# One attention-plus-two-layers kernel: conversion jobs in another order, more filler transposes at the start, the last product's operands split in place

## Chip, cores and metric

The kernel runs on one core of one Trainium2 chip. The metric is device time in microseconds; the time before is the median of three runs, 1113.74 us (1110.79 to 1116.33).

## What is computed

The reference is attention with rotary embedding, then a gated layer with a norm in front, then a second layer without a nonlinearity. Shapes: batch 4, 8 heads, 576 positions, 64 per head; 2304 tokens of width 512; inner widths 1536 and 1024.

```
q_rot, k_rot = rotate(q), rotate(k)
attn = softmax(q_rot @ k_rot.T / sqrt(64)) @ v            # 32 heads
x  = attn as [2304, 512]
xn = x / sqrt(mean(x*x) + 1e-6) * rms_g
x2 = (silu(xn @ w_gate) * (xn @ w_val)) @ w_out            # gated layer
h  = (x2 @ w1) * (x2 @ w2) @ w3                            # second layer
out = h @ w_out2
```

All inputs are double-width words, of which the kernel makes 32-bit floats itself. Each operand of a product is split into a high part (rounded to the multiplier's format) and a low part (the remainder), and every product is three passes: high·high, high·low, low·high (`PASS`).

## The kernel before

**Start and attention.** A core has TensorE (PE, with its weight loads PEld), VectorE (DVE), ScalarE (ACT), GpSimd (POOL), and SyncE (SP), whose one queue issues all the DMAs. The work goes by 16 pairs of heads; pair 0's start is written out by hand (lines 705 to 753). `warm(i)` issues `WARM[i]` transposes of the identity into a bank that nobody reads: 22 before anything else, 2 after the transposes `q2p` of the rotated keys, 3 after `q0p`. Then come `q1p`, the splits into `xy`, copies into `ks` and `qs`, and the first scores (L495). ACT takes the exponential (L506) after DVE's maximum (L500). The keys and queries of pair 1 go into `ks` and `qs` by DMA (`move`, L447). The order in attention is a table (`ORDER`, `ONCE`) and is not touched.

**Gated layer.** The tokens go in six chunks of 384. A step is one slice of 128 inner columns of one chunk: 24 matmuls into `mm` (L307), then ACT's silu `sg` (L317), DVE's product `u` (L319), and the split of `u` into `us`, high by ACT (L106), low by DVE (L107). The 12 matmuls that add `us` times `w_out` into `acc` (L828) come one step later. Chunks 0 and 1 convert the layer's own weights; from chunk 2 on DVE, ACT and SP prepare the second layer in **jobs**, which the list `JOBS` hangs on steps (i, n), chunk and slice:

- `job_wo` (8 of them): load 512 KB of `w_out2`, convert (`conv`: one ACT step L856, three DVE steps L857, L860, L861), split by ACT and DVE, store two parts in `woD`.
- `job_w3` (16): load, convert, store one part in `w3D`.
- `job_ws` (8): convert `w1` or `w2` and store sums of blocks in `wsD` for a seven-product scheme.
- `job_sums` (4): read two chunks' `x2` back, form block sums, split them, store in `xsD`. Its `xo` tiles are in the pool `x2` of three buffers, which the tiles `xr` of the norm (of the next chunk) and the results `x` share.

A job's load is issued a step or more ahead of its work. A scheduler sets the order of each engine's queue from the program's order, dependencies and modelled times; DVE, ACT and SP then take their queues strictly in order.

**Second layer and end.** Stage L1064 forms the seven products per block; its chains of matmuls add into a bank that ACT (L1070 to L1078) or DVE (L1054) must read in between. Its operands `xs` leave the pools `xsA` and `xsB` as the last blocks finish. Into the freed slots go `woc` (`w_out2`, both parts, from `woD`). `w3_trans` transposes a block of `w3` (L1156) and splits it (L106, L107); `w3_prod` multiplies it with all eight `woc` (L1167) and splits the result into `wp`. Then `load_us` loads the layer's `u` from `uD` into a `gv` tile and splits it into `us`, chunk by chunk, and L1205 makes the output of a chunk in 72 matmuls. `load_us(0)` stands after all eight `w3_prod`.

Of the kernel before, what the change touches and what calls it, by code (L numbers as in the profile page):

```python
# [8 lines left out]
F32 = mybir.dt.float32  # L9
# [31 lines left out]
WARM = (22, 2, 3, 17)  # L41
# [8 lines left out]
JOBS = ([(2, 0, ("wo", 0)), (2, 1, ("wo", 1))] + [(2, 3 + j, ("wo", j)) for j in range(2, 8)] + [(2, 11, ("w3", 0, 0))]  # L50
        + [(3, j // 2 if j < 10 else j - 5, ("w3", (j + 1) // 2, (j + 1) % 2)) for j in range(15)]
        + [(i, 2 + c, ("sums", i // 2 - 1, c)) for i in (2, 4) for c in range(2)]
# [10 lines left out]
def f(ap):  # L63
    return ap.bitcast(F32)
# [3 lines left out]
def kernel(  # L68
# [56 lines left out]
    woD = dram.tile([128, NJ, 2, DM], F32, name="woD")  # L125
# [598 lines left out]
    def warm(i):  # L724
        for _ in range(WARM[i]):
            nc.tensor.transpose(wps[:, 0:128], idn, idn)
# [10 lines left out]
    for i, n_ in enumerate(("q2p", "q0p", "q1p")):  # L737
        part[n_](0)
        if i < 2:
            warm(i + 1)  # L740
# [128 lines left out]
    def job_wo(j):  # L869
        load, rest = conv(rows(w_out2, j))  # L870

        def go():
            t = rest()
            hi, lo = [wt_p.tile([128, 512], F32R, tag="t", name="wt") for _ in range(2)]
            split(hi, lo, t)
            for i, o in enumerate((hi, lo)):
                nc.sync.dma_start(out=woD[:, j, i], in_=f(o))
        return [load, go]
# [150 lines left out]
    def gtile(shape, dt=F32):  # L1029
        return gv.tile(shape, dt, tag="g", name="gv")  # L1030
# [141 lines left out]
    def load_us(i):  # L1172
        us = []
        for g in range(NJ // 2):
            t = gtile([128, 2, CH])
            nc.sync.dma_start(out=t, in_=uD[:, 2 * g:2 * g + 2, i * CH:(i + 1) * CH])
            o = (xsA if i else xsB).tile([128, 2, 2, CH], F32R, tag="x", name="us")
            split(o[:, 0], o[:, 1], t)
            us.append(o)
        return us  # L1180
# [3 lines left out]
    for j in range(NJ):  # L1184
        woc[j] = (xsA if j < 7 else xsB).tile([128, 2, 512], F32R, tag="x", name="woc")
        nc.sync.dma_start(out=f(woc[j]), in_=woD[:, j])
    w3_trans(0)
    for j in range(NJ):
        if j + 2 < NJ:
            w3_load(j + 2)  # L1190
        if j + 1 < NJ:
            w3_trans(j + 1)
        w3_prod(j)


    nus = load_us(0)
# [74 lines left out]
```

## Time and profile before

| what | value |
|---|---|
| median of three runs | 1113.74 us (1110.79 to 1116.33) |
| the profiled execution's own time | 1111.08 us |
| its span in the trace | 1109.3 us |
| PE busy | 1075.6 us (97%) |
| DVE busy | 685.0 us (62%) |
| ACT busy | 558.2 us (50%) |
| POOL busy | 242.8 us (22%) |
| DMA, mean over the span | 165 GB/s |

The span is the profiled execution from its first to its last instruction; 1.8 us of its time lie around it. Shares of busy time are means over stages. Attention takes the span up to some 300 us, the gated layer from there to 775 us, the seven-product stage to 960 us, the last products the rest. In the trace's views a line is "start, length, engine, line, operation, out<-in, count", and what stands in brackets is the idle time ahead of it and what ended that.

### The profile page before, as it was taken

What the parts mean: (1) busy time and instruction counts of PE and PEld (TensorE: products, weight loads), DVE (VectorE), ACT (ScalarE), POOL (GpSimd) and SP (SyncE); (2) the same over time, 40 slices, a digit from 0 to 9 for tenths busy, and PEclk for the clock granted to TensorE, in tenths of its full rate; (3) what the DMA queues carried; (4) which work ended last, traced back from release to release, by engine and by line L of the source; (5) the groups of instructions that cost most, each with busy time, mean ns of one, the idle gap of its engine ahead of it and who ended that gap; (6) DMA issues with size and microseconds to landing.
All of it is one profiled execution on the core that took longest, in us unless ns stands there. A gap on an engine that the chain in (4) does not pass through costs nothing. (4 is left out here: it accounts for less than half of the span.)

```text
span 1109.3 us, 18452 instructions
## 1 busy us (share of the span) xinstructions
PE 1075.6 (97%) x6627; PEld 1036.1 (93%) x6627; DVE 685.0 (62%) x1278; ACT 558.2 (50%) x1241; POOL 242.8 (22%) x359
## 2 busy tenths in 40 slices
PE   6899999999899999999999999999999999999998
PEld 6899999999889999999999999999899999887886
DVE  6899999999889853452677566552363442423320
ACT  5799998998865533232533343233353433223230
POOL 5878898799300000000000000000000000000000
PEclk8999999999999999999999999999999999999999
DMA  7678867776356531151978685636932416604451
GB/s 201 168 179 205 211 173 187 197 195 149 85 181 182 170 95 58 41 169 43 310 242 286 213 285 197 219 101 206 349 112 71 134 72 197 221 15 127 143 171 57
DMA packets 124699, 183.53 MB, mean 165 GB/s; under 512 B 18624, under 2 KB 85696, under 8 KB 124608
## 3 DMA queue, kind: packets, MB, share of 16 engines
q1 hardware_dynamic: 124608, 182.35, 54.1%
q8 instruction: 53, 0.87, 0.3%
q14 instruction: 38, 0.31, 0.1%
HBM read 101.63 MB, written 52.17 MB: 139 GB/s over the span
## 5 line engine op out<-in xcount | busy, mean ns | idle before, releaser
L307 PE MATMUL mm<-xc,wgv 128*128 128x384 f32 x1728 | 316.4, 335 | 0.9 <-ACT sg L317 0.5
L307 PEld LDWEIGHTS mm<-xc,wgv 128*128 128x128 f32 x1728 | 299.9, 188 | 1.8 <-ACT wgv L244 0.9
L1064 PE MATMUL ps<-xs,cw 128*128 128x384 f32 x1008 | 176.5, 335 | 2.2 <-DMA xs<-xsD 2.2
L1064 PEld LDWEIGHTS ps<-xs,cw 128*128 128x128 f32 x1008 | 174.5, 188 | 3.6 <-DMA xs<-xsD 2.9
L828 PE MATMUL acc<-us,wo 128*128 128x384 f32 x864 | 167.3, 336 | 4.5 <-ACT us L106 2.6
L828 PEld LDWEIGHTS acc<-us,wo 128*128 128x128 f32 x864 | 150.6, 188 | 7.8 <-ACT us L106 4.2
L495 PE MATMUL s<-ks,qs 128*128 128x288 f32 x640 | 122.6, 319 | 10.8 <-ACT osb L573 5.6
L500 DVE TENSOR_REDUCE nm<-s 128x1 f32<-128x576 f32 x144 | 107.9, 749 | 10.8 <-PE s L495 9.0
L506 ACT ACTIVATE p<-s,nm 128x576 f32<-128x576 f32 x144 | 107.5, 747 | 12.8 <-DVE nm L500 12.2
L495 PEld LDWEIGHTS s<-ks,qs 128*128 128x128 f32 x640 | 91.9, 194 | 14.0 <-ACT osb L573 5.6
L1205 PE MATMUL ps<-wp,us 128*128 128x512 f32 x432 | 98.2, 389 | 1.4 <-ACT us L106 1.4
L1205 PEld LDWEIGHTS ps<-wp,us 128*128 128x128 f32 x432 | 81.0, 188 | 18.6 <-ACT us L106 1.8
L520 DVE TENSOR_TENSOR pt<-tp,pt 128x512 fp32r<-128x512 f32 x144 | 94.5, 681 | 1.2 <-ACT pt L516 0.6
L319 DVE SCALAR_TENSOR_TENSOR u<-mm,sg 128x384 f32<-128x384 f32 x72 | 39.8, 553 | 78.2 <-PE mm L307 70.4
L106 ACT CAST us<-u 128x384 fp32r<-128x384 f32 x72 | 36.8, 511 | 101.4 <-DVE u L319 101.1
L568 PE MATMUL pv<-pt,vs 128*128 128x288 f32 x512 | 81.0, 300 | 2.7 <-DVE pt L520 2.7
L516 ACT CAST pt<-tp 128x512 fp32r<-128x512 f32 x144 | 82.5, 585 | 1.4 <-PE tp L512 0.5
L512 PE MATMUL tp<-idn,p 128*128 128x128 f32 x576 | 82.1, 275 | 0.1
L568 PEld LDWEIGHTS pv<-pt,vs 128*128 128x128 f32 x512 | 70.8, 188 | 3.2 <-DVE pt L520 3.2
L512 PEld LDWEIGHTS tp<-idn,p 128*128 128x128 f32 x576 | 67.9, 142 | 1.4 <-issue 0.4
L317 ACT ACTIVATE sg<-mm 128x384 f32<-128x384 f32 x72 | 35.1, 488 | 54.9 <-PE mm L307 54.6
L1054 DVE TENSOR_TENSOR gv<-ps,gv 128x384 f32<-128x384 f32 x48 | 26.7, 556 | 53.5 <-PE ps L1064 33.4
(138 smaller groups left out, 1368.3 us busy)
## 6 DMA issues: line engine op xcount, KB each, us to landing
ks<-xy SPq DMA_DIRECT2D x62, 288.0 KB, 5.0
wraw<-in_moe_w_dram SPq DMA_DIRECT2D x32, 512.0 KB, 5.1
xsD<-xo SPq DMA_DIRECT2D x28, 384.0 KB, 3.6
xs<-xsD SPq DMA_DIRECT2D x14, 768.0 KB, 8.6
wraw<-in_moe_w_out_dram SPq DMA_DIRECT2D x20, 512.0 KB, 4.4
qs<-xy SPq DMA_DIRECT2D x62, 160.0 KB, 2.8
uD<-gv SPq DMA_DIRECT2D x12, 768.0 KB, 3.7
gv<-uD SPq DMA_DIRECT2D x24, 384.0 KB, 4.5
```

What stands on the lines that cost most here:

```text
L307: nc.tensor.matmul(ps[:, 0:CH], lhsT=w[:, a, s, c * 128:(c + 1) * 128], rhs=x[:, b_, c, :], start=(i == 0), stop=(i == 3 * KC - 1))
L319: nc.vector.scalar_tensor_tensor(out=u, in0=va, scalar=1.0 / UP, in1=sg, op0=ALU.mult, op1=ALU.mult)
L495: nc.tensor.matmul(ps[:, hf, 0:HS], lhsT=l, rhs=r_[:, hf * HS:(hf + 1) * HS], start=(i == 0), stop=(i == n - 1))
L500: nc.vector.tensor_reduce(out=nm, in_=s_ps[p, t][:, :, 0:HS], axis=AX.XY, op=ALU.max, negate=True)
L506: nc.scalar.activation(out=pp.rearrange("p (a b) -> p a b", a=2), in_=s_ps.pop((p, t))[:, :, 0:HS], func=AF.Exp, bias=s_max.pop((p, t)), s ...
L512: nc.tensor.transpose(ps[:, c, :], p_sb[p, t][:, LF + c * 128:LF + (c + 1) * 128], idn)
L516: lastins["act"] = nc.scalar.copy(out=hi, in_=src)
L520: lastins["dve"] = nc.vector.tensor_tensor(out=lo, in0=src, in1=f(hi), op=ALU.subtract)
L568: nc.tensor.matmul(ps[:, 0:HS], lhsT=l.rearrange("p s d -> p (s d)"), rhs=r, start=(i == 0), stop=(i == 8))
L828: nc.tensor.matmul(acc[o][:, 0:CH], lhsT=wo[kind, n][:, a, o * 128:(o + 1) * 128], rhs=us[:, b_], start=(n == first and s == 0), stop=(n = ...
L1064: nc.tensor.matmul(b[ch], lhsT=w[i][:, p_, c * 128:(c + 1) * 128], rhs=x[i][:, r, c], start=(first and ch != 1 and n == 0), stop=(n == 5), ...
L1205: nc.tensor.matmul(ac[o], lhsT=us[j // 2][:, a, j % 2, o * 128:(o + 1) * 128], rhs=wp[j][:, b_], start=(j == 0 and s == 0), stop=(j == NJ ...
```

## The change

1. `WARM` goes from (22, 2, 3, 17) to (22, 18, 3, 26), and `warm(3)`, which was never called, now follows `q1p`.
2. `JOBS` is another list. The eight `wo` and the first ten `w3` jobs have their loads in chunk 2, one or two a step, with the work one step later; `sums` of chunks 0 and 1 move from chunk 2 to steps 1 to 4 of chunk 3; the last `w3` jobs come in steps 5 to 11 of chunk 3. The `ws` jobs and the second `sums` stay.
3. `job_wo` no longer splits: it stores one converted part, and `woD` is half as large. At the end, `woc` loads that part into a third plane of its tile and splits it there.
4. `load_us` loads straight into the `us` tile and splits in place, without a `gv` tile; `load_us(0)` moves ahead of the sixth `w3_prod`.

```diff
-WARM = (22, 2, 3, 17)
+WARM = (22, 18, 3, 26)
...
-JOBS = ([(2, 0, ("wo", 0)), (2, 1, ("wo", 1))] + [(2, 3 + j, ("wo", j)) for j in range(2, 8)] + [(2, 11, ("w3", 0, 0))]
-        + [(3, j // 2 if j < 10 else j - 5, ("w3", (j + 1) // 2, (j + 1) % 2)) for j in range(15)]
-        + [(i, 2 + c, ("sums", i // 2 - 1, c)) for i in (2, 4) for c in range(2)]
+JOBS = ([(i, n, ("wo", j) if j < 8 else ("w3", (j - 8) // 2, j % 2)) for j, (i, n) in enumerate(
+            [(2, n) for n, k in enumerate((1, 2, 2, 2, 2, 1, 2, 1, 2, 1, 1, 1)) for _ in range(k)]
+            + [(3, n) for n in (0, 5, 6, 9, 10, 11)])]
+        + [(3, 1 + 2 * c, ("sums", 0, c)) for c in range(2)] + [(4, 2 + c, ("sums", 1, c)) for c in range(2)]
...
-    woD = dram.tile([128, NJ, 2, DM], F32, name="woD")
+    woD = dram.tile([128, NJ, DM], F32, name="woD")
...
-        if i < 2:
-            warm(i + 1)
+        warm(i + 1)
...
-        def go():
-            t = rest()
-            hi, lo = [wt_p.tile([128, 512], F32R, tag="t", name="wt") for _ in range(2)]
-            split(hi, lo, t)
-            for i, o in enumerate((hi, lo)):
-                nc.sync.dma_start(out=woD[:, j, i], in_=f(o))
-        return [load, go]
+        return [load, lambda: nc.sync.dma_start(out=woD[:, j], in_=rest())]
...
-            t = gtile([128, 2, CH])
-            nc.sync.dma_start(out=t, in_=uD[:, 2 * g:2 * g + 2, i * CH:(i + 1) * CH])
             o = (xsA if i else xsB).tile([128, 2, 2, CH], F32R, tag="x", name="us")
-            split(o[:, 0], o[:, 1], t)
+            nc.sync.dma_start(out=f(o[:, 1]), in_=uD[:, 2 * g:2 * g + 2, i * CH:(i + 1) * CH])
+            split(o[:, 0], o[:, 1], f(o[:, 1]))
...
-        woc[j] = (xsA if j < 7 else xsB).tile([128, 2, 512], F32R, tag="x", name="woc")
-        nc.sync.dma_start(out=f(woc[j]), in_=woD[:, j])
+        woc[j] = (xsA if j < 7 else xsB).tile([128, 3, 512], F32R, tag="x", name="woc")
+        nc.sync.dma_start(out=f(woc[j][:, 2]), in_=woD[:, j])
+    for j in range(NJ):
+        split(woc[j][:, 0], woc[j][:, 1], f(woc[j][:, 2]))
     w3_trans(0)
     for j in range(NJ):
+        if j == NJ - 3:
+            nus = load_us(0)
...
-    nus = load_us(0)
```

What moves in the engines' queues is shown at three places.

**PE at the start**, before and then after (`warm` is the filler, `qtp` the transposes of pair 0's keys and queries, `s` its first scores):

```order
L726 MATMUL warm<-idn 128x128 x22
L429 MATMUL qtp<-idn,rot 128x128 x4
L726 MATMUL warm<-idn 128x128 x2
L429 MATMUL qtp<-idn,rot 128x128
L726 MATMUL warm<-idn 128x128 x3
L429 MATMUL qtp<-idn,rot 128x128 x4
L495 MATMUL s<-ks,qs_139 128x288 x16
```

```order
L727 MATMUL warm<-idn 128x128 x22
L430 MATMUL qtp<-idn,rot 128x128 x4
L727 MATMUL warm<-idn 128x128 x18
L430 MATMUL qtp<-idn,rot 128x128
L727 MATMUL warm<-idn 128x128 x3
L430 MATMUL qtp<-idn,rot 128x128 x4
L727 MATMUL warm<-idn 128x128 x26
L496 MATMUL s<-ks,qs_139 128x288 x16
```

Sixteen more fillers stand ahead of the second group of transposes and 26 ahead of the first scores.

**DVE in the gated layer where conversions are densest**: before in chunk 3, between two products `u` (the `u` ahead of these rows stands one L857 earlier); then after, in chunk 2, between two products `u` (`wraw` and `wt` are a job's tiles, `nt`, `rstd` and `xr` the norm's):

```order
L672 TENSOR_TENSOR nt<-nt,ms 128x3
L860 SCALAR_TENSOR_TENSOR wt<-wraw 128x512
L673 TENSOR_TENSOR nt<-cst,nt 128x3
L860 SCALAR_TENSOR_TENSOR wt<-wraw 128x512
L107 TENSOR_TENSOR us<-u,us 128x384
L861 SCALAR_TENSOR_TENSOR wt<-wraw,wt 128x512
L674 TENSOR_TENSOR rstd<-rstd,nt 128x3
L861 SCALAR_TENSOR_TENSOR wt<-wraw,wt 128x512
L857 TENSOR_SCALAR wraw<-wraw 128x512
L683 SCALAR_TENSOR_TENSOR xr<-xr,rstd,g 128x512 x3
L860 SCALAR_TENSOR_TENSOR wt<-wraw 128x512
L319 SCALAR_TENSOR_TENSOR u<-mm,sg 128x384
```

```order
L320 SCALAR_TENSOR_TENSOR u<-mm,sg 128x384
L675 TENSOR_TENSOR rstd<-rstd,nt 128x3
L684 SCALAR_TENSOR_TENSOR xr<-xr,rstd,g 128x512 x3
L108 TENSOR_TENSOR us<-u,us 128x384
L857 TENSOR_SCALAR wraw<-wraw 128x512 x2
L860 SCALAR_TENSOR_TENSOR wt<-wraw 128x512 x2
L861 SCALAR_TENSOR_TENSOR wt<-wraw,wt 128x512 x2
L320 SCALAR_TENSOR_TENSOR u<-mm,sg 128x384
L108 TENSOR_TENSOR us<-u,us 128x384
```

Before, the steps of three or more conversions, the norm's and one `us` stand between the two `u`; after, those of two conversions, the norm's and one `us`.

**ACT at the end of the seven-product stage**, before and then after (`gv<-ps 128x384` and `ps<-ps` are the reads of a chain's bank, `gv<-ps 128x512` the split of a transposed `w3` block):

```order
L1074 COPY gv<-ps 128x384
L1070 COPY ps<-ps 128x384
L1074 COPY gv<-ps 128x384
L1078 COPY gv<-ps 128x384 x2
L1072 COPY gv<-ps 128x384
L106 CAST gv<-ps 128x512 x2
L1074 COPY gv<-ps 128x384
L106 CAST gv<-ps 128x512 x2
L1078 COPY gv<-ps 128x384
```

```order
L107 CAST woc<-woc 128x512
L1067 COPY gv<-ps 128x384
L107 CAST us<-us 128x768
L1063 COPY ps<-ps 128x384
L107 CAST us<-us 128x768
L107 CAST woc<-woc 128x512
L1067 COPY gv<-ps 128x384
L1071 COPY gv<-ps 128x384
L107 CAST us<-us 128x768
L107 CAST woc<-woc 128x512 x2
L1071 COPY gv<-ps 128x384
L1065 COPY gv<-ps 128x384
```

The reads of the chains' banks now stand behind steps on `woc` and `us`, each of which waits for a load.

## Rows read from the trace of the kernel before

**Rows 1.** The page: busy time and share of TensorE.

```profile
PE 1075.6 (97%) x6627; PEld 1036.1 (93%) x6627; DVE 685.0 (62%) x1278; ACT 558.2 (50%) x1241; POOL 242.8 (22%) x359
```

**Rows 2.** Waits of PE from 480 to 780 us: total, times, longest.

```profile
PE acc L828 <- ACT us L106: 2.0, 2, 1.0
PE acc L828 <- DVE us L107: 1.5, 3, 0.8
PE mm L307 <- ACT sg L317: 0.5, 1, 0.5
```

**Rows 3.** Timeline of PE, 560 to 780 us: the last of these waits.

```profile
677.22 2.62 PE L828 MATMUL acc<-us,wo 128*128 128x384 f32 x12 [0.93 <-ACT us L106]
```

**Rows 4.** Waits of SP's queue, 470 to 625 us.

```profile
SPq L953 <- DVE xo L107: 45.4, 11, 31.2
```

**Rows 5.** Groups by line, 470 to 625 us: busy, mean ns, idle before.

```profile
L860 DVE SCALAR_TENSOR_TENSOR wt<-wraw 128x512 uint32<-128x512 uint32 x25 | 17.1, 689 | 3.5 <-ACT wraw L856 1.8 <-DMA woD<-wt 1.1
L319 DVE SCALAR_TENSOR_TENSOR u<-mm,sg 128x384 f32<-128x384 f32 x24 | 13.3, 554 | 20.4 <-PE mm L307 18.1 <-ACT xo L106 2.0
L857 DVE TENSOR_SCALAR wraw<-wraw 128x512 uint32<-128x512 uint32 x24 | 10.1, 426 | 10.3 <-DMA wraw<-in_moe_w_dram 8.4 <-DMA wraw<-in_moe_w_out_dram 1.9
L106 ACT CAST us<-u 128x384 fp32r<-128x384 f32 x24 | 12.2, 510 | 23.0 <-DVE u L319 23.0
```

**Rows 6.** The chain that ended last: products of one step.

```profile
620.13 4.16 PE mm L307 x24
```

**Rows 7.** Waits of DVE, 550 to 625 us.

```profile
DVE wraw L857 <- DMA wraw<-in_moe_w_dram: 8.4, 9, 1.9
```

**Rows 8.** Timeline of PE, 0 to 45 us.

```profile
1.36 4.95 PE L726 MATMUL warm<-idn 128*128 128x128 f32 x22 [1.36 <-POOL idn masks.py:199]
...
7.46 0.38 PE L726 MATMUL warm<-idn 128*128 128x128 f32 x2
9.93 0.33 PE L429 MATMUL qtp<-idn,rot 128*128 128x128 f32 x1 [2.09 <-POOL rot L396]
...
14.68 2.26 PE L495 MATMUL s<-ks,qs 128*128 128x288 f32 x8 [3.11 <-DVE qs L749]
...
20.96 1.31 PE L495 MATMUL s<-ks,qs 128*128 128x288 f32 x8
...
34.01 1.12 PE L495 MATMUL s<-ks,qs 128*128 128x288 f32 x4 [3.83 <-ACT osb L573]
```

**Rows 9.** Stretches of 2 us: length, busy PE PEld DVE ACT POOL, PEclk, DMA share, GB/s.

```profile
10.00:12.00 2.00, 1.57 (x8) 1.17 (x8) 1.37 (x2) 1.33 (x3) 2.00 (x3) 0.58 0.07 16
...
22.00:24.00 2.00, 2.00 (x19) 1.98 (x19) 1.91 (x5) 1.92 (x6) 0.53 (x1) 1.00 1.07 372
```

**Rows 10.** The DMAs of `ks` issued from 27.6 to 28.7 us.

```profile
L447 SPq DMA_DIRECT2D ks<-xy x2: 617/1140/1662, 27.9 to 28.6; - x2
...
DMA to landing us min/median/max: 5.7/6.0/6.3
```

**Rows 11.** Timeline, all engines, 36 to 62 us: transposes in attention.

```profile
54.65 1.47 PE L512 MATMUL tp<-idn,p 128*128 128x128 f32 x12
```

**Rows 12.** Timeline, all engines, 915 to 1012 us: the end of the seven-product stage.

```profile
949.47 0.48 ACT L1072 COPY gv<-ps 128x384 f32<-128x384 f32 x1 [0.90 <-PE ps L1064]
...
951.87 1.29 PE L1064 MATMUL ps<-xs,cw 128*128 128x384 f32 x6
...
954.43 3.02 PE L1167 MATMUL ps<-woc,gv 128*128 128x512 f32 x12 [0.37 <-DVE gv L107]
...
1005.51 2.29 ACT L106 CAST us<-gv 128x768 fp32r<-128x768 f32 x3
...
1006.38 5.96 PE L1205 MATMUL ps<-wp,us 128*128 128x512 f32 x25 [1.41 <-ACT us L106]
```

**Rows 13.** SP's queue, 925 to 965 us.

```profile
946.34 0.32 SPq L1186 DMA_DIRECT2D woc<-woD  x1
```

**Rows 14.** Loads of `w3c` (256 KB each), 910 to 965 us.

```profile
DMA to landing us min/median/max: 2.6/3.3/6.2
```

## The prediction, made before the change was run

> **What bounds the kernel now.** I read the page first: PE is busy 97% of the span [rows 1], so only 1109.3 - 1075.6 = 33.7 us of the span are left to win, plus what a low clock makes PE's work longer. Then I read who PE waits for, stage by stage, and at each such place the timeline and the other engines' queues. Three places bear on the change.
>
> In the gated layer PE waits 4.0 us between 480 and 780 us, nearly all of it for `us` or `sg`, that is for DVE and ACT to finish a step's small work [rows 2]; 0.93 of that is at 677 us, among the `ws` jobs, which do not move [rows 3]. The other 3.07 lie in chunk 3, where the conversions are dense. Why they are dense there can be read on SP: its queue stood 45.4 us, once 31.2 at a stretch, before a store of `xo` that DVE had not made yet [rows 4]; the loads of the later jobs were behind it. The `xo` and the norm's `xr` take turns in the same three buffers.
>
> At the start, PE makes its first fillers and goes idle 2.09 us before `q0p` and 3.11 us before the first scores [rows 8]. Between 10 and 12 us the granted clock is 0.58 of full, so it falls to 1.2 GHz there [rows 9], and eight first scores take 2.26 us where eight later ones take 1.31 [rows 8].
>
> At the end, PE stands 1.41 us before the last product because ACT first splits `us` [rows 12].
>
> **The start.** Sixteen more fillers go into the 2.09 us gap and 26 into the 3.11 us gap. Twelve transposes at full clock took 1.47 us in attention, 0.12 each [rows 11]; so 18 take some 2.2 us and end at 9.7, before `q0p` can start at 9.93 [rows 8], and 26 take 3.2 us, about the gap ahead of the scores. They cost nothing by themselves as long as the clock is full; that DVE's `qs` ends the wait for the scores [rows 8] is their cover. If the clock stays at 2.4 GHz, the first eight scores save 2.26 - 1.31 = 0.95 us, and the second eight as much: up to 1.9 us. But that is not the end of it: PE stands idle 3.83 us before the first scores of pair 1 at 34.01 [rows 8], and what comes just before them is a DMA into `ks`, issued at 27.9 at the earliest and 5.7 us under way, so landing at about 33.6 [rows 10]. The row names ACT's `osb`, but the landing is as near. From 22 us on the DMA engines are full (share 1.07 [rows 9]), so an earlier issue does not land much earlier. Most of the 1.9 us becomes a longer idle time at 30 to 34 us. The lower bound is all 1.9 saved, the upper bound stands under the rivals. I take **-0.5**, nearer to nothing because the DMA row is the nearer limit.
>
> **The jobs.** Each `wo` job loses an ACT step, a DVE step of the size of L860 (0.69 us) and one of two stores. That work is off PE's path and counts only where it delays `us`. What matters is the room. The 24 matmuls of a step take 4.16 us [rows 6]; with the 12 of the same size into `acc`, a step lasts 6.24. From the end of a step's products to `us` go `sg`, `u`, the high part and the low part, four pieces of about 0.51 to 0.55 us [rows 5], 2.1 in all, and `us` is needed 6.24 later: room of some 4.1 us. What DVE does from one `u` to the next beyond 6.24 us makes `u` late. Before, in the queue shown, that is five steps like L860 (0.69), two L857 (0.43) [rows 5], three norm steps of L860's shape and one `us`: 6.9 us, and three conversions wait for loads that land up to 1.9 us late each [rows 7]: 12.6 at worst, 6.4 late, more than the room; the step after it is as dense. After, the densest stretch between two `u` is two conversions, 2 x (0.43 + 0.69 + 0.69) = 3.6, the norm's steps and one `us`: 6.4 us, and two loads that may be late: 10.2 at worst, 4.0 late, which the room just covers; the steps beside it are lighter. In chunk 3 the sums go with only six conversions. The second sums were made in chunk 4 before, and of the six waits in rows 2 only that of [rows 3] lies there.
>
> So of the 3.07 us I let one wait of the longest length seen, 1.0 [rows 2], stay, and take **-2.1**. The bounds are -3.07 (none stays) and 0 (all of it moves to chunk 2, which now has 18 conversions). SP is passed by eight fewer stores, and its long stand before `xo` should go, since the sums end before the norm loads its tiles.
>
> **The end.** `load_us(0)` ahead of the sixth `w3_prod` makes `us` ready long before 1006; the 1.41 us go. New are eight ACT steps and eight DVE steps on `woc`, and four and four on `us`, in the queues that read the chains' banks. All wait for loads. The last `woc` is issued at 946.34 [rows 13]. It is now half as large, 256 KB, as the `w3c` loads are, which took 3.3 us in the median, 2.6 at best and 6.2 at worst [rows 14]. So it lands at 949.6; ACT's copy (about 0.6, by the 0.51 for 384 columns [rows 5]) and two bank reads of 0.48 behind it end at 951.2, and PE needs the bank read at 949.47 before its six matmuls at 951.87 [rows 12]: covered, by 0.7 us. Behind it on DVE stand two `woc` steps of about 0.69 and what they push back, ahead of the low part of the first transposed block, for which PE already waited 0.37 us at 954.43 [rows 12]. I take 1.0 us there. Splitting in place adds no work for `us`; the loads now wait for the slots of `woc`, which the last `w3_prod` frees some 16 us before chunk 1 needs them (72 matmuls, where 25 take 5.96 [rows 12]). Sum **-1.41 + 1.0 = -0.4**. Bounds: -1.8 (both waits gone), and +6.2 if landings are late, worked out below.
>
> For one DMA, the Trainium skill (DMA: Bandwidth & Descriptors, Anatomy of one DMA) gives about 2.0 us plus the bytes at 436 GB/s. That is an estimate of 2.6 us for 256 KB; by it no ACT or DVE step here is late and the end is worth -1.4. The median row, 3.3, is longer, and it decides; the rule's case is in the first rival.
>
> **Sum**: -0.5 - 2.1 - 0.4 = -3.0 us. The profiled execution took 1111.08 us, 2.66 below the median of its three runs; put on the median, 1113.74 - 3.0 = **1110.7 us**.
>
> **Rivals.**
>
> *All waits go.* Pair 1's scores follow the earlier start (-1.9), no conversion is late (-3.07), the splits at the end are hidden (-1.41 - 0.37). That is -6.75, 1107.0. For it: loads do land in 2.6 [rows 14], and the denser DVE stretches before were denser than anything now. Against: the landing of `ks`, and late landings in every stretch.
>
> *The waits move to chunk 2.* DVE has 18 conversions there beside the part sums of chunk 0, and PE waits as long as before: -0.5 - 0.4 = -0.9, 1112.8.
>
> *The fillers run at 1.2 GHz* (slower). If the clock has fallen by 7.5 us, a filler takes 4.95 / 22 = 0.225 us [rows 8]: 18 end at 11.5, 1.6 after `q0p` could start, and 26 take 5.9 us in a gap of 3.11, 2.7 too long. The first scores come 4.3 us later, and if the 3.83 us idle ahead of pair 1 hide none of it, the sum is 4.3 - 2.1 - 0.4 = +1.8, 1115.5. It decides from the point where fillers end after 14.6 us. Against it: the fillers follow the transposes at 7.46 at once, where before 2.09 us without work lay ahead of the low clock [rows 8, 9].
>
> Of that gate the Trainium skill (TensorE: Matmul & The Clock Gate, Part 1: The HAM clock gate) says that its moment is not tied to the kernel's start and differs between runs; by that this rival would come in some executions and not in others. No trace here shows it.
>
> *Late landings at the end* (slower). If `woc` and `us` land as the worst row, 6.2 us [rows 14], each of the three places where a bank read stands behind them is late by 2.9 - 0.7 = 2.2: 6.6 in all, and the sum is -0.5 - 2.1 - 1.41 + 6.6 + 1.0 = +3.6, 1117.3. It begins to cost at landings over 4.0 us.
>
> **Chances.** Forecast 0.50, all go 0.20, waits move 0.15, fillers slow 0.07, late landings 0.08. Runs of one kernel lie up to 2.9 us below and 2.6 above their median, so the range goes from below the first rival, 1105.0, to above the second, 1116.3; the tails of the two slower ones are left out. The forecast's own range is 1108.3 to 1113.3. A measurement can tell about 0.5% from no change, 5.6 us: faster by that means under 1108.2, which takes most of the first rival and the forecast's lower tail, 0.25; slower means over 1119.3, the late landings with a little more, 0.08; the same 0.67.
>
> **What would show it.** Right: the granted clock at full from 7 us through the first scores, eight of them in about 1.3 us, and still an idle time of 3 to 5 us before pair 1's scores; no stand of SP of tens of us in chunk 2; PE's waits for `us` and `sg` from 480 to 780 down from 4.0 to some 1.9; none before L1200 at about 1003, and a wait of some 1.4 before the first L1160. Wrong: pair 1's scores starting over a microsecond earlier (the DMA was no limit), waits of PE in chunk 2 of 3 us, or PE waiting for ACT between 935 and 955 us.

## The result, and the profile after

The changed kernel takes **1102.34 us** in the median (1101.56 to 1103.68, four runs) beside 1113.64 us before (1110.79 to 1116.33, four runs): ratio 0.990, interval 0.9873 to 0.9927. That is 11.3 us less. The forecast was 3.0 us less, and the time lies below its range, which ended at 1105.0. A second set of runs gave 1101.29 beside 1112.81, ratio 0.9893 (0.987 to 0.9916).

The two profiled executions lie only 7.4 us apart (1103.68 and 1111.08 us): the one after is the slowest of its four, the one before lies 2.6 under its median. What differs between executions of the same kernel is therefore part of the question below.

The page after, busy times:

```profile
PE 1077.5 (98%) x6669; PEld 1040.8 (94%) x6669; DVE 680.4 (62%) x1278; ACT 557.0 (51%) x1241; POOL 243.3 (22%) x359
```

PE is busy 1.9 us longer than in [rows 1], with 42 fillers more, and the span falls from 1109.3 to 1101.9.

**The gated layer.** All waits of PE from 480 to 780 us, where [rows 2] had six of 4.0 us in all:

```profile
PE acc L828 <- ACT us L107: 1.5, 1, 1.5
```

One is left, at the place of [rows 3]. SP's waits from 470 to 625 us for a store of `xo`, the 45.4 us of [rows 4]:

```profile
SPq L946 <- DVE xo L108: 12.9, 12, 3.3
```

The long stand is gone too. The waits lay in chunk 3, from its first product to the first of chunk 4. These are the rows of PE's timeline at both points, before and then after:

```profile
539.04 1.20 PE L307 MATMUL mm<-xc,wgv 128*128 128x384 f32 x6
...
619.97 1.20 PE L307 MATMUL mm<-xc,wgv 128*128 128x384 f32 x6
```

```profile
538.60 1.72 PE L308 MATMUL mm<-xc,wgv 128*128 128x384 f32 x9
...
614.82 1.37 PE L308 MATMUL mm<-xc,wgv 128*128 128x384 f32 x7
```

Chunk 3 took 619.97 - 539.04 = 80.93 us and takes 76.22, which is 4.71 less, though its listed waits came to some 3.0. A listed wait is only part of what a stall costs, as these rows of the kernel before show, from the middle of its chunk 3:

```profile
576.03 2.01 PE L828 MATMUL acc<-us,wo 128*128 128x384 f32 x10 [0.78 <-DVE us L107]
...
584.58 1.89 PE L828 MATMUL acc<-us,wo 128*128 128x384 f32 x10
...
595.50 0.34 PE L828 MATMUL acc<-us,wo 128*128 128x384 f32 x1
596.36 2.18 PE L828 MATMUL acc<-us,wo 128*128 128x384 f32 x11 [0.52 <-DVE us L107]
```

One product is listed with 0.34 us, but without a stall the next one starts 0.17 us later (24 in 4.16 us [rows 6]). Across the last of these waits the starts lie 0.86 us apart, so that 0.69 us are lost where 0.52 are listed. And ten products behind a wait take 2.01 us, where ten without one take 1.89. That is some 0.3 us more for each of the five waits in chunk 3, an estimate of 1.4 of the 1.7 us that the list lacks.

Chunk 2 went the other way, from 76.22 to 77.07.

**The start.** PE's timeline after, for [rows 8], and the granted clock of three stretches (the number after the last engine's busy time), two of them those of [rows 9]:

```profile
6.80 2.13 PE L727 MATMUL warm<-idn 128*128 128x128 f32 x18
9.71 0.33 PE L430 MATMUL qtp<-idn,rot 128*128 128x128 f32 x1 [0.78 <-POOL rot L397]
...
10.64 3.00 PE L727 MATMUL warm<-idn 128*128 128x128 f32 x26
13.95 1.29 PE L496 MATMUL s<-ks,qs 128*128 128x288 f32 x8 [0.31 <-DVE qs L749]
...
18.95 1.33 PE L496 MATMUL s<-ks,qs 128*128 128x288 f32 x8
...
32.97 1.30 PE L496 MATMUL s<-ks,qs 128*128 128x288 f32 x4 [4.81 <-DMA ks<-xy]
...
35.87 2.76 PE L513 MATMUL tp<-idn,p 128*128 128x128 f32 x12
...
44.17 0.77 PE L496 MATMUL s<-ks,qs 128*128 128x288 f32 x4
```

```profile
10.00:12.00 2.00, 2.00 (x21) 2.00 (x20) 1.59 (x3) 1.86 (x4) 2.00 (x3) 1.00 0.10 24
22.00:24.00 2.00, 1.94 (x16) 1.50 (x13) 1.97 (x4) 2.00 (x6) 0.36 (x1) 1.00 1.08 369
34.00:38.00 4.00, 4.00 (x20) 3.80 (x18) 3.52 (x5) 2.35 (x5) 4.00 (x5) 0.50 0.52 149
```

The gaps are filled, the clock holds, and eight first scores take 1.29 us, as forecast. The scores that stood at 20.96 us come at 18.95, 2.0 us earlier. But PE then stands 4.81 us where it stood 3.83, now with the landing of `ks` named, and behind that the clock is at 1.2 GHz (0.50): twelve transposes take 2.76 us, against 1.47 at full clock [rows 11]. Before, the clock was low there for part of the time too, and these twelve took 1.91 us. At 44 us nothing of the gain is left in this execution; the kernel before came to the same scores here:

```profile
44.02 0.77 PE L495 MATMUL s<-ks,qs 128*128 128x288 f32 x4
```

**The end.** The last product begins without a wait, at 999.13 instead of 1006.38; the first product with `woc` waits 0.76 us, where [rows 12] had 0.37 at that stage:

```profile
947.45 0.73 PE L1160 MATMUL ps<-woc,gv 128*128 128x512 f32 x2 [0.76 <-ACT gv L107]
...
993.69 5.60 PE L1160 MATMUL ps<-woc,gv 128*128 128x512 f32 x24
999.13 3.11 PE L1200 MATMUL ps<-wp,us 128*128 128x512 f32 x13
```

From the first product of the seven-product stage to the last product took 231.08 us before and 229.05 after. Of these 2.0 us some 1.0 is a wait for `xs` at 786 us, which took 0.2 to 2.6 us in the profiled executions of whatever kernel.

### The profile page after: what moved, and what is told of

Read it like the earlier page. It is cut to its first block, busy times and chain, and to the rows that moved or that the text cites. A ratio compares the mean times of both kernels' runs of the same rounds, so it can differ in the third digit from the quotient of the medians.

```text
span 1101.9 us, 18536 instructions
## 1 busy us (share of the span) xinstructions
PE 1077.5 (98%) x6669; PEld 1040.8 (94%) x6669; DVE 680.4 (62%) x1278; ACT 557.0 (51%) x1241; POOL 243.3 (22%) x359
## 4 chain that ended last, share of the span: by engine, by line
PE 72%; DMA 11%; POOL 6%; DVE 5%; issue 2%; SPq 2%; ACT 1%; POOLq 0%; DVEq 0%; ACTq 0%
PE mm L308 22%; PE ps L1057 13%; PE acc L828 11%; PE ps L1200 9%; PE ps L1160 4%; PE s L496 4%; PE pv L569 3%; PE tp L513 3%; POOL rtmp L383 2%; DMA raw<-in_q_dram 2%; POOL rot L377 2%; DMA x2D<-x 1%; DMA vr<-in_v_dram 1%; DMA ks<-xy 1%; DMA xs<-xsD 1%
## 5 line engine op out<-in xcount | busy, mean ns | idle before, releaser
L320 DVE SCALAR_TENSOR_TENSOR u<-mm,sg 128x384 f32<-128x384 f32 x72 | 39.8, 553 | 86.1 <-PE mm L308 80.9
L108 DVE TENSOR_TENSOR us<-u,us 128x384 fp32r<-128x384 f32 x72 | 40.0, 556 | 36.3 <-ACT us L107 36.2
```

## The experiments

All of them in one table: median, ratio to the kernel before in the same set of runs with its interval, median of the mean granted clocks of its runs, and of its profiled execution the start of the gated layer and the lengths of chunks 2 and 3. A chunk has 288 products into `mm`; its length is the time from its first to the first of the next chunk, as above. All times in us. In the sets of runs below the kernel before took 1112.71 (beside e1 to e4), 1111.58 (e5 to e8), 1112.81 (e9 to e12), 1112.19 (e13 to e16) and 1112.25 (e17, e18); the clock in its row is that of its 23 runs beside e1 to e4.

| kernel | median | ratio, interval | clock | gated layer begins | chunk 2 | chunk 3 |
|---|---|---|---|---|---|---|
| before | 1113.64 | 1 | 0.991 | 309.5 | 76.2 | 80.9 |
| changed | 1102.34 | 0.990 (0.9873 to 0.9927) | 0.996 | 308.8 | 77.1 | 76.2 |
| e1_warm | 1106.95 | 0.995 (0.9932 to 0.9969) | 0.996 | 308.0 | 76.6 | 82.0 |
| e2_jobs | 1110.87 | 0.9976 (0.9957 to 0.9995) | 0.992 | 311.6 | 79.6 | 76.2 |
| e3_wo | 1106.34 | 0.9941 (0.992 to 0.9963) | 0.990 | 309.7 | 76.2 | 76.4 |
| e4_us | 1111.92 | 0.9995 (0.9977 to 1.0012) | 0.991 | 310.9 | 76.2 | 82.1 |
| e5_warm0 | 1104.39 | 0.9935 (0.9909 to 0.9961) | 0.991 | 308.7 | 76.3 | 76.2 |
| e6_jobs0 | 1102.51 | 0.9921 (0.9896 to 0.9947) | 0.996 | 311.1 | 76.2 | 76.2 |
| e7_wo0 | 1103.01 | 0.9926 (0.9902 to 0.995) | 0.996 | 307.5 | 79.1 | 76.2 |
| e8_us0 | 1101.95 | 0.9915 (0.9888 to 0.9943) | 0.996 | 306.6 | 76.8 | 76.2 |
| e9_after | 1101.29 | 0.9893 (0.987 to 0.9916) | 0.996 | 306.3 | 76.3 | 76.2 |
| e10_warm0 | 1106.53 | 0.9944 (0.9919 to 0.9969) | 0.990 | 311.8 | 76.2 | 76.2 |
| e11_in_place | 1109.16 | 0.9966 (0.9945 to 0.9986) | 0.991 | 311.3 | 76.2 | 79.7 |
| e12_fill | 1106.29 | 0.9952 (0.9932 to 0.9972) | 0.998 | 305.5 | 81.6 | 76.2 |
| e13_pool | 1110.45 | 0.999 (0.997 to 1.001) | 0.990 | 311.2 | 76.2 | 79.7 |
| e14_fill_old_list | 1103.38 | 0.9922 (0.9898 to 0.9945) | 0.998 | 305.7 | 76.2 | 78.7 |
| e15_gap1 | 1104.05 | 0.9934 (0.9913 to 0.9955) | 0.992 | 307.8 | 76.2 | 76.2 |
| e16_gap2 | 1106.01 | 0.994 (0.9918 to 0.9963) | 0.992 | 308.8 | 76.2 | 76.2 |
| e17_raw | 1112.22 | 0.9998 (0.9981 to 1.0015) | 0.990 | 310.1 | 76.2 | 82.4 |
| e18_two_parts | 1103.26 | 0.9908 (0.9878 to 0.9938) | 0.997 | 307.1 | 76.2 | 77.2 |

The theory at the outset (A) was that the jobs carry most of the gain, as the two traces say. Its rivals: the start is worth more than the two profiled executions show (B), and what made room is the split that the `wo` jobs lost, not the list (C).

### Each part alone

**e1_warm**: the fillers.

```diff
-WARM = (22, 2, 3, 17)
+WARM = (22, 18, 3, 26)
...
-        if i < 2:
-            warm(i + 1)
+        warm(i + 1)
```

> The kernel before with the fillers of the change alone (22, 18, 3, 26). Theory A (the start is nearly worth what the two profiles show: the gated stage began 0.67 us earlier): -0.5 to -1 against before, some 1113 us, and before's own spread of 5.5 us stays. Rival B (the 3.9 us by which the medians differ more than the two profiled executions lie in the start, whose low clock falls at other moments in other executions): -4 to -5, some 1109 us, and a spread of about 2 us.

1106.95, 5.8 us less: rival B by size. The clock of its runs is 0.995 to 0.997, where 23 runs of the kernel before in the same set had 0.987 to 0.994, 0.991 in the median. Its own spread stayed at 4.5 us where rival B had some 2, so executions differ nearly as much without the low clock at the start.

**e2_jobs**: the new `JOBS` alone, the jobs' code as before.

```diff
-JOBS = ([(2, 0, ("wo", 0)), (2, 1, ("wo", 1))] + [(2, 3 + j, ("wo", j)) for j in range(2, 8)] + [(2, 11, ("w3", 0, 0))]
...
+JOBS = ([(i, n, ("wo", j) if j < 8 else ("w3", (j - 8) // 2, j % 2)) for j, (i, n) in enumerate(
...
```

> The kernel before with the new list JOBS alone; the wo jobs still split and store two parts. Theory A (the jobs carry the largest part; in the two profiles the stretch 340 to 775 us became 3.9 us shorter): -3 to -4.7, some 1109.5 us. Rival C (it is the removed split and store of the wo jobs that made room, the list only moves the load): 0 to +2, the waits for us then stand in chunk 2. Rival B: as A at most -1.

1.8 us less. The waits of chunk 3 are gone, and these stand in chunk 2 instead (PE's waits from 470 to 560 us):

```profile
PE acc L829 <- ACT us L107: 1.4, 1, 1.4
PE acc L829 <- DVE us L108: 0.6, 2, 0.4
```

By position chunk 2 lost 3.4 us and chunk 3 won 4.7. The time alone, between the expected ones, does not decide; by the trace theory A fell here: the list by itself moves the waits. It is the rival "the waits move to chunk 2" of the prediction, in a kernel in which the split is still there.

**e3_wo**: `w_out2` stored once and split at the end, old list.

```diff
...
-            t = rest()
-            hi, lo = [wt_p.tile([128, 512], F32R, tag="t", name="wt") for _ in range(2)]
-            split(hi, lo, t)
-            for i, o in enumerate((hi, lo)):
-                nc.sync.dma_start(out=woD[:, j, i], in_=f(o))
+            nc.sync.dma_start(out=woD[:, j], in_=rest())
...
-        nc.sync.dma_start(out=f(woc[j]), in_=woD[:, j])
+        nc.sync.dma_start(out=f(woc[j][:, 2]), in_=woD[:, j])
+    for j in range(NJ):
+        split(woc[j][:, 0], woc[j][:, 1], f(woc[j][:, 2]))
```

> The kernel before with the converted w_out2 stored once and split at the end, in a third plane of woc; old list of jobs, old fillers, old load_us. Theory A: at most -1, since the waits of chunk 3 lie among the w3 jobs, whose list stays; at the end 0 to +1 for the bank reads behind the splits of woc. Rival C (the removed steps made the room): -3 or more.

6.4 us less, rival C. PE has no wait at all from 535 to 625 us and chunk 3 takes 76.4 us, with the old list. And SP still stands as long before `xo`:

```profile
SPq L946 <- DVE xo L107: 44.3, 10, 29.1
```

So the long stand of [rows 4], which the prediction took for the reason that the conversions are dense, is not what makes PE wait. What the view of DVE's waits from 470 to 560 us had in the kernel before is this, and it is missing here:

```profile
DVE wt L107 <- DMA woD<-wt: 3.5, 3, 1.7
```

The split's two results and the converted part take all three `wt` buffers, and DVE, whose queue is in order, stood for the landing of a store.

**e4_us**: `load_us` in place and ahead of the sixth `w3_prod`, alone.

```diff
-            t = gtile([128, 2, CH])
-            nc.sync.dma_start(out=t, in_=uD[:, 2 * g:2 * g + 2, i * CH:(i + 1) * CH])
-            split(o[:, 0], o[:, 1], t)
+            nc.sync.dma_start(out=f(o[:, 1]), in_=uD[:, 2 * g:2 * g + 2, i * CH:(i + 1) * CH])
+            split(o[:, 0], o[:, 1], f(o[:, 1]))
...
+        if j == NJ - 3:
+            nus = load_us(0)
...
-    nus = load_us(0)
```

> The kernel before with load_us split in place and its first chunk loaded ahead of the sixth w3_prod alone. Theory A: -1.41 for the wait that goes and up to -0.4 more, some 1112 us. Rival D (the end is worth more than its listed wait, since the loads of us no longer meet the loads of the blocks): -3. A loss of 1 or more would say that the bank reads stand behind the splits of us.

Within the noise of no change (0.9977 to 1.0012), which does not exclude 1.4 us but does exclude rival D's 3. In its trace the 1.41 us before the last product are gone and the wait at L1167 is 0.9 instead of 0.4.

### The change without one part

From the changed kernel one of the four edits above is taken back at a time, each the diff of e1, e2, e3 or e4 with its signs turned: the fillers in **e5_warm0**, the list in **e6_jobs0**, the `wo` jobs in **e7_wo0**, `load_us` in **e8_us0**.

> The changed kernel with the old fillers. Theory A' (after the first four runs: the fillers save low-clock time, 10 us less of it by the clocks of the runs, worth half of that where PE is busy): +5, some 1107 us, mean clock of its runs back to .988 to .993. Rival (the fillers' gain in the first run was chance, the traces show 0.7 to 1.5 us): +0.5 to +1.5.

> The changed kernel with the old list of jobs (wo jobs without the split). Theory E (the removed split made the room, the new list adds nothing to it): 0 within 1 us, no waits for us or sg in chunk 3 though SP still stands some 30 us before xo. Theory A (the list does it): +3 to +4, the waits of chunk 3 back.

> The changed kernel with the old wo jobs, which split and store two parts; new list, fillers and load_us. Theory E: +2 to +4, with waits for us in chunk 2 as in the run of the new list alone (2.0 us listed, 3.4 by position). Theory A (the list is the cause): +0.5 or less.

> The changed kernel with the old load_us, through a gv tile and after the last w3_prod. +1.4 to +1.8, since the wait before the last product returns. Rival (the early loads and splits cost elsewhere what they save there): within 0.5 of the changed kernel.

The changed kernel was not in this set, so these four are set beside its two ratios, 0.990 and 0.9893; by the intervals such a difference is good to some 4 us. With the old fillers (e5) the clock is back at 0.988 to 0.992 and the ratio is 0.9935, some 4 to 5 us above the changed kernel: theory A'. With the old list (e6) there is no wait of PE from 460 to 640 us, while SP stands 45.6 us before `xo`, 30.2 at a stretch: theory E by the trace, since once the split is gone the list takes nothing more from chunks 2 and 3. The median, 2 to 3 us above the changed kernel by ratio, lies between the theories and does not decide. With the split back (e7) chunk 2 is 79.1, as in e2, and the ratio 0.9926, some 3 to 4 us: theory E. With the old `load_us` (e8) the wait is back in the trace:

```profile
996.43 5.96 PE L1200 MATMUL ps<-wp,us 128*128 128x512 f32 x25 [1.41 <-ACT us L107]
```

Its 1.4 us can be seen there and not in the medians, whose runs differ by more.

### The size of the fillers' part

**e9_after** is the changed kernel again, without an edit, and **e10_warm0** the same with the diff of e1 taken back, both on one chip.

> The changed kernel once more, beside the kernels of this set on one chip. By the first timing 0.987 to 0.993 of before; by the lengths of the stages in the traces (attention -1.7 in the mean of five and five, chunks 2 and 3 -4.5, the end -1.4 to -2) -8, 0.993.

> The changed kernel with the old fillers, again, now beside the changed kernel itself. Theory T (the traces are right on the fillers: the gated layer begins 1.7 us earlier with them in the mean of five and five executions): +1.7 against the changed kernel, at most +2.5. Theory M (the median of the fillers alone is right): +5, at least +3.4.

1101.29 and 1106.53: 5.2 us, theory M. Two estimates from rows and clocks stand beside that. By the clocks, 0.990 and 0.996 over some 1105 us, the low clock (half speed) lasts 2 x 1105 x 0.010 = 22 us with the old fillers and 2 x 1105 x 0.004 = 9 with the new; eight scores take 2.26 instead of 1.31 us at low clock [rows 8], so that 42% of 13 us or 5.5 us are lost, if PE has work throughout. It has not: in every one of these traces it stands 2.1 to 6.1 us ahead of pair 1's first scores. By the traces, the gated layer begins at 310.5 us in the mean of the nine kernels with the old fillers (308.7 to 311.8) and at 307.9 in the mean of the seven with both gaps filled and none added (306.3 to 311.1): 2.6 us. The profiled executions with the old fillers lie 0.8 us under their medians in the mean and the others 0.6 above, 1.4 more. The rest of the difference is within the spread of executions; one trace of each kernel does not settle it.

Where the 2.6 us come about can be read in the same sixteen traces, by position (the 151st product is counted without fillers):

| mean of, us | PE goes idle ahead of pair 1 | pair 1's first scores | 151st product | PE's listed waits from there to the gated layer | gated layer begins |
|---|---|---|---|---|---|
| nine with the old fillers | 30.7 | 34.2 | 43.0 | 6.4 (5.6 to 7.8) | 310.5 |
| seven with the new | 28.4 | 33.5 | 42.7 | 4.1 (3.0 to 4.4, and one 7.4) | 307.9 |

The wait ahead of pair 1 takes most of what the start wins: of 2.3 us 0.7 are left at its first scores and 0.2 at 43 us. Nor does it show there how long the clock was low: of the nine traces five have some 14 us of low clock at the start and four some 10, and pair 1's scores begin at 34.2 and 34.1 us. The gain comes later, in PE's waits for results of ACT and DVE; the two traces have this one, before and then after, over the whole span:

```profile
PE op L582 <- DVE pt L520: 1.7, 2, 1.0
```

```profile
PE op L583 <- DVE pt L521: 0.4, 1, 0.4
```

Why these waits become shorter was not tried. That the fillers save the time is shown by e1 and by e10 beside e9; the way from the fillers to the 5 us is not.

The windows of e10 and then of e9 at the start (the clock is the number after five busy times):

```profile
12.00:15.00 3.00, 0.61 (x2) 0.65 (x3) 2.09 (x3) 1.38 (x3) 3.00 (x5) 0.50 0.96 193
15.00:20.00 5.00, 4.25 (x18) 3.88 (x18) 2.48 (x4) 2.11 (x5) 5.00 (x8) 0.50 0.67 173
20.00:24.00 4.00, 4.00 (x22) 3.98 (x21) 2.03 (x4) 2.56 (x7) 2.23 (x3) 0.57 0.92 296
```

```profile
12.00:15.00 3.00, 2.69 (x24) 2.48 (x23) 2.08 (x4) 1.15 (x2) 3.00 (x4) 1.00 0.89 181
15.00:20.00 5.00, 3.70 (x26) 3.08 (x25) 3.23 (x5) 3.19 (x8) 5.00 (x8) 1.00 0.74 182
20.00:24.00 4.00, 3.94 (x34) 3.69 (x32) 3.88 (x8) 3.88 (x11) 2.66 (x4) 1.00 0.86 266
```

With the old fillers the clock stays low to 23 us here; in the execution of [rows 9] it was full again by 22. Between 20 and 24 us PE makes 22 products in one and 34 in the other.

**e15_gap1, e16_gap2**: one gap filled, the other left.

```diff
-WARM = (22, 18, 3, 26)
+WARM = (22, 18, 3, 2)       (e15)
+WARM = (22, 2, 3, 26)       (e16)
```

> The changed kernel with the first gap filled and the second left idle (22, 18, 3, 2). If the clock falls in any idle gap of 3 us: low clock from some 13 us through the first scores, +2 to +5 against the changed kernel. If the first gap alone started the low clock before: 0 to +1.

> The changed kernel with the second gap filled and the first left idle (22, 2, 3, 26). The clock falls at some 10 us as before, so the 26 fillers take some 5.9 us at 1.2 GHz in a gap of 3 us: the first scores come at 16.5 to 17 us instead of 14.3. If the wait for ks at 34 hides that: +3 to +5, as with the old fillers. If not: +6 to +8.

1104.05 and 1106.01, ratios of 0.9934 and 0.994 like those with neither gap filled and within the ranges expected: one filled gap gives nothing that these medians show, both give the 5 us. (Their traces do not say why: from 43 us to the gated layer their listed waits are 4.3 and 3.6 us, like those with both gaps filled.) In e15 the clock falls within the 2.9 idle us ahead of the first scores and is at 0.50 from 15 to 20 us. In e16 the rival "fillers at 1.2 GHz" can be seen in part:

```profile
9.71 0.33 PE L430 MATMUL qtp<-idn,rot 128*128 128x128 f32 x1 [2.24 <-POOL rot L397]
...
10.64 4.67 PE L727 MATMUL warm<-idn 128*128 128x128 f32 x26
15.06 1.29 PE L496 MATMUL s<-ks,qs 128*128 128x288 f32 x8
```

The clock fell behind the first gap (0.60 from 12 to 15 us) and was full again at 15: 26 fillers took 4.67 us, not 5.9, and the scores came at 15.06, not at 16.5 to 17.

### What in the split costs the time

Three kernels keep the split of the kernel before and change one thing of it.

e11_in_place makes the low part in place:

```diff
-            hi, lo = [wt_p.tile([128, 512], F32R, tag="t", name="wt") for _ in range(2)]
+            hi, lo = wt_p.tile([128, 512], F32R, tag="t", name="wt"), t.bitcast(F32R)
```

e13_pool makes it on GpSimd:

```diff
-            split(hi, lo, t)
+            split(hi, lo, t, nc.gpsimd)
```

e17_raw writes both parts into the job's load tile:

```diff
-            raw = u["raw"]
+            raw = conv.raw = u["raw"]
...
-            hi, lo = [wt_p.tile([128, 512], F32R, tag="t", name="wt") for _ in range(2)]
+            raw = conv.raw.rearrange("p n t -> p (n t)").bitcast(F32R)
+            hi, lo = raw[:, 0:512], raw[:, 512:1024]
```

> The kernel before; the wo jobs still split with the same ACT and DVE steps and the same two stores, but the low part is made in place, so that a job holds two of the three wt buffers and not three. Theory F (DVE's work was held up by the turn of the buffers, 3.5 us of waits for the stores of woD in chunk 2 and 1.1 in chunk 3): the waits of chunk 3 shrink, it takes 77 to 79 us instead of 80.9, some 1109 to 1111 us in all. Theory G (it is the volume of the split's steps and stores): chunk 3 stays within 1 us of 80.9.

> The kernel before; the wo jobs still split, with the same three wt buffers and two stores, but the eight low parts are made by GpSimd, which has no other work then. Theory G (DVE's own eight steps of 0.69 us fill its queue): chunk 3 falls to 76 to 77.5 us, some 1108 us. Theory F (the turn of the buffers and the stores): chunk 3 stays at 79.5 or more, within 2 us of before.

> The kernel before; the wo jobs still split, with the same ACT and DVE steps and the same two stores, but both parts are written into the job's own load tile, so that a job holds one wt buffer as after the change. Theory F (the turn of the wt buffers): no wait of DVE for a store of woD in wt, chunk 3 at 76.2 to 77.5, some 1108 us. Theory G (volume of steps and stores): chunk 3 at 79 or more. Either way the load tiles are held longer, which may move waits to the loads.

Chunk 3 takes 79.7, 79.7 and 82.4 us, where the three kernels with the old list and the old split have 80.9, 82.0 and 82.1 (before, e1, e4). Two buffers a job instead of three: 1.3 us of the 4.7 (3.7 less in the median). Eight DVE steps fewer, made by GpSimd: also 1.2 in the trace, 0.1% in the median; DVE waited 7.9 us for GpSimd to free a buffer. One `wt` buffer a job, with the load tiles held instead: nothing. There the waits for stores moved to the load tiles:

```profile
DVE wraw L857 <- DMA woD<-wraw: 3.9, 1, 3.9
```

By their expectations e11 stands between the theories, e13 speaks for F and e17 for G, so neither is shown alone. The split as a whole (a step on ACT and on DVE, two buffers held for a store's landing, a second store) is what makes PE wait in chunk 3, and taking it out whole frees 4.6 us there; how that divides stays open. More `wt` buffers were not tried.

### More fillers, and the two parts that matter

**e12_fill**: 30 more fillers ahead of pair 1's first scores, into their own bank; **e14_fill_old_list**: the same with the diff of e2 taken back, that is with the old list.

```diff
+            if p == 1 and not any(k[0] == 1 for k in p_sb) and not any(k[0] == 1 for k in s_ps):
+                for _ in range(30):
+                    nc.tensor.transpose(ps[:, 0, 0:128], idn, idn)
```

> The changed kernel with 30 more fillers, into the bank of pair 1's first scores ahead of them, where PE now stands 4.8 us for the landing of ks and the clock falls for 6.8 us. If low clock costs there what the rows show (some 7.5 us of PE work from 32.97 that takes 4.4 at full clock): -3, and no low clock until 200 us. If ACT and DVE set the pace behind the scores there: -0.5 to 0. If the fillers end after the landing: 0 to +1.

> The changed kernel with the old list of jobs and 30 fillers ahead of pair 1's scores. If the fillers are worth what the stretch up to the gated layer showed (305.5 us against 306.3 to 308.8 in two executions of the changed kernel) and the old list has no late us in chunk 2: 1098 to 1100, 1 to 3 under the changed kernel. If their time is lost in chunk 2 here too, 1104 to 1106 with chunk 2 at 80 or more.

The clock holds through the wait for `ks`, as the rows after it show:

```profile
29.12 3.49 PE L490 MATMUL s<-idn 128*128 128x128 f32 x30 [0.85 <-ACT p L510]
33.22 0.77 PE L499 MATMUL s<-ks,qs 128*128 128x288 f32 x4 [0.60 <-issue]
...
34.79 1.47 PE L516 MATMUL tp<-idn,p 128*128 128x128 f32 x12
```

The gated layer begins at 305.5 and 305.7 us, earlier than in any other kernel. But neither beats the changed kernel: e12 is 5.0 us slower than e9 beside it, which none of its three expectations had, and e14, at 1103.38, lies between its two and cannot be told from the changed kernel. In the trace of e12 chunk 2 takes 81.6 us with the same queues. ACT's timeline, then DVE's and PE's, show how:

```profile
485.26 0.63 ACT L682 ACTIVATE xc<-xr 128x512 fp32r<-128x512 f32 x1 [4.08 <-DMA xr<-xD]
485.80 0.19 ACT L682 ACTIVATION_READ_ACCUMULATOR xc<-xr 128x1 f32 x1
485.89 0.49 ACT L107 CAST us<-u 128x384 fp32r<-128x384 f32 x1
```

```profile
486.42 0.56 DVE L108 TENSOR_TENSOR us<-u,us 128x384 fp32r<-128x384 f32 x1 [6.22 <-ACT us L107]
```

```profile
498.23 3.74 PE L831 MATMUL acc<-us,wo 128*128 128x384 f32 x11 [1.98 <-DVE us L108]
```

The norm's load `xr` landed 1.8 us later than in e9 (at 485.2 instead of 483.4), and `us` stands behind it in ACT's queue; a load of `w3` was late next. Then eleven products take 3.74 us, at low clock (0.57 in the mean from 498 to 502 us). In e14 chunk 3 takes 78.7 with 1.3 us of waits for `us`. So in e12 `us` stands behind a load that came late. One trace does not show whether that comes of reaching this place earlier, or in most executions.

**e18_two_parts**: the kernel before with the fillers and the `wo` jobs of the change (the diffs of e1 and e3), nothing else.

> The kernel before with two of the four parts: the fillers, and w_out2 stored once and split at the end. Old list, old load_us. If these two carry the gain: -5.5 and -5, some 1101 to 1102, within 1.5 us of the changed kernel (the 1.4 us ahead of the last product remain). If the list or the early load_us is needed as well: 1104 or more.

1103.26, ratio 0.9908 beside 0.990 and 0.9893 of the whole, between the two expectations: these two parts carry the gain to within 1 or 2 us.

## Why the prediction was wrong

The signs were right and two sizes were not.

- **The start**, forecast -0.5, measured -5.2 (e10 beside e9) and -5.8 (e1), and some 4 to 5 by the ratio of e5. The step that failed is the bound, "The lower bound is all 1.9 saved": it ends the account of the fillers at pair 1's first scores and puts at nothing, without a reason, what they change in the rest of attention. The step before it, "Most of the 1.9 us becomes a longer idle time at 30 to 34 us", holds: in the means of nine and seven traces 2.3 us are won, and 0.2 of them are left at 43 us. (In the two profiled executions pair 1's scores come 1.04 us earlier, just over the microsecond that was named as a sign of being wrong.) What the runs show in its place is that PE's listed waits from 43 us to the gated layer fall from 6.4 to 4.1 us, and that the gated layer begins 2.6 us earlier. Why, and where the rest of the 5 us lies, stays open.
- **The jobs**, forecast -2.1 with a bound of -3.07, measured -4.7 in chunk 3 and up to +0.85 in chunk 2. Two steps failed. The price: the bound was the sum of listed waits, and by position chunk 3 lost 1.6 times as much, and chunk 2 in e2 1.7 times (3.4 us for 2.0 listed). The reason: the list was held to thin the conversions out and SP's stand to make them dense; e3 and e6 show that without the split the old list has no waits there, with the stand in place (e18 has one of 0.4 us), and e2 that the list without the removed split only moves them. The removal of an ACT and a DVE step, with what hangs on them, was written down as the smaller part ("That work is off PE's path") and is the larger.
- **The end**, forecast -0.4, measured -1.0 when the difference in the wait for `xs` is left out: the 1.41 us went, as e8 shows by their return. The loss of 1.0 for the `woc` splits measured 0.4 in the profiled execution (0.76 instead of 0.37). That 0.76 is a wait for ACT between 935 and 955 us, which the prediction had named as a sign of being wrong, though it had also priced a wait of 1.4 there. In the nine kernels that split `woc` at the end and load `us` early, PE waits 0.8 to 2.0 us for the split blocks of `w3` in the profiled executions, 1.3 in the mean, so that 1.0 more was about right.
- **The rivals.** "All waits go" had the right direction, 1107.0, and lacked the same two sizes. "The waits move to chunk 2" is true of the list alone (e2, e7). "Fillers at 1.2 GHz" comes about in part, and only when the first gap is left open (e16). "Late landings" do not show at the end, where `woc` landed after 2.8 to 4.1 us, but in chunk 2 of e12, which is 5.3 us longer than in e9, a place that the prediction did not name. The rule of the Trainium skill ("TensorE: Matmul & The Clock Gate", Part 1: The HAM clock gate) that the moment of the clock's change differs between runs was used for the fillers alone. The traces agree with it: in the nine with the old fillers the first low stretch begins anywhere from 8.8 to 11.2 us and lasts some 10 or 14. It was not what made the price of the start wrong, since pair 1's scores begin alike behind both.

The measured 11.3 us are then, by the single runs, some 5 for the fillers and 6 for the removed split (e1 and e3; 9.0 for the two together in e18). By the traces they are 2.6 up to the gated layer, 4.7 in chunk 3 less 0.85 in chunk 2, and 1 at the end; the other 3.9 us are not placed by the traces.

## What to carry to other kernels

An earlier start is not priced by the next wait alone: follow it by position through the rest of its stage, and in several traces, since attention took 308.8 us in one execution of the changed kernel and 306.3 in another. The list of waits bounds a stall from below; take the distance between two products of the same kind, over the whole stage, for its price. When work is moved and also shrunk, try each alone: here the shrinking did it, and the new order only moved the waits.

## What was not expected of the hardware

- Short idle times at the start were followed by long low clock: behind 2.1 and 3.1 idle us [rows 8] it stood at 1.2 GHz for 10 to 14 us. Yet hardly any of that could be seen at 43 us, behind the 2.1 to 6.1 us that PE stood ahead of pair 1 in between.
- Less low clock is not by itself less time: e12 runs at 0.998, above the changed kernel's 0.996, and is 5.0 us slower in its median. In its trace it begins the gated layer 0.8 us earlier than e9 and loses 5.3 us in chunk 2.
- A wait of PE is followed by further loss that no row lists as idle: 3.0 us listed cost 4.7, 2.0 cost 3.4.
